# Polysketch attention and a four-expert mix: the first chunk of 128 columns multiplied plainly, and a reordered beginning

**Chip, cores, metric.** One core of a Trainium2 chip. Times are microseconds (us) of device time for one execution. A time quoted for a kernel is the median of its runs. All runs count as fast ones unless a run is called slow. In the lines of the profile PE is TensorE, PEld its loading of weights, DVE VectorE, ACT ScalarE and POOL GpSimd.

## The reference

```python
q, k, v: (4, 4, 1088, 32)      # batch, heads, sequence, head dim
S1, S2:  (8, 32)
domain_probs: (4352, 4);  w1: (4, 128, 1024);  w2: (4, 1024, 128)

phi(x) = outer(S1 x, S2 x)                    # 64 features of each row
kv, z  = phi(k)^T v, sum of phi(k)            # one set for each head
x      = (phi(q) kv) / (phi(q) z + 1e-6)      # heads side by side: (4352, 128)
p      = domain_probs / (domain_probs.sum(-1) + 1e-9)
out    = sum over e of p[:, e] * (relu(x @ w1[e]) @ w2[e])
```

## The kernel before

The 4352 columns of x (transposed: xT is 128 x 4352) are made in units of attention work and used in chunks of expert work. A chunk has 16 steps: 4 experts, each in 4 steps of 256 hidden rows. The engines work as follows.

- **TensorE** multiplies by w1, then two steps later by w2. It also does the attention's projections.
- **ScalarE** does the ReLU from PSUM to SBUF.
- **VectorE** does the subtractions that the second multiplication needs, and all the small steps of the attention.
- **GpSimd** makes the weight sums w2s and gathers the results.

```python
UNITS  = [[256, 416, 416]] + [[384, 352, 352]] * 3         # attention, by batch
CHUNKS = [256, 416, 416] + [512] * 5 + [320, 256, P]       # expert work
ps_h: 3 PSUM buffers "h";  ps_o: "o0", "o1";  ps_f: one "f";  ps_n: "den", "num"
```

All chunks but the last use a scheme of seven half-width products in place of eight. That costs three subtractions a step on VectorE, and four weight sums for each expert on GpSimd:

```python
# first(i): one step of expert e
for j in range(2):
    both(hp, w1[e, ...], xT[chunk])                        # TensorE
    nc.scalar.activation(hd[...], hp, Relu)                # ScalarE
    rectify_and_subtract(...)                              # VectorE: one for j = 0, two for j = 1
    work()
# second(i): seven products of w2 blocks or w2s with the parts of hd
# the last chunk, plain(m): only a transposing Relu, and eight records of 128 columns
```

The next units' attention is a generator of small "pieces". `work()` puts them between the expert steps, at a rate that has each chunk's columns ready in time. The pieces of the queries, in their order:

```python
# queries(b, c, n): transpose of q ... projection into the PSUM buffer "f"
qf = shuffle(f); qf = f + qf                               # VectorE
qb = shuffle(qf)
for x in range(2):
    qa = shuffle(qf)
    for p in range(2):
        qp[p] = qa * qb                                    # VectorE, two SBUF inputs
# attend: den, num on TensorE; transpose, add, reciprocal, transpose, product on VectorE
```

At the beginning, the sketch words S1 and S2 (64-bit numbers) are taken apart on VectorE (19 small operations) and spread by ScalarE and VectorE to `sk` (for keys) and by GpSimd to `sr` (for queries). The keys are transposed, projected and summed, and the first unit's 256 columns pass the attention. Only then can the first expert matmul start.

## Time and profile before

| | before |
|---|---|
| time, median of 3 | 500.53 us (500.36 to 500.74) |
| profiled span | 498.2 us |
| TensorE busy | 98% |
| first key projection / first expert matmul | 6.43 / 16.96 us |

The page, the windows up to 94.72 and the opening are in the prediction below. What belongs to them here are the later windows of the kernel before (from:to, length; then busy time and count of TensorE, weight loads, VectorE, ScalarE, GpSimd; granted clock, DMA share, GB/s):

```profile
140.42:197.61 57.19, 57.19 (x511) 42.40 (x509) 39.07 (x81) 28.30 (x54) 23.25 (x23) 1.00 0.18 52
197.61:478.82 281.21, 281.21 (x2325) 211.84 (x2323) 182.59 (x422) 148.41 (x293) 139.21 (x141) 1.00 0.08 22
```

and its timeline in chunk 1 (start, length, engine, line, operation, out<-in, count; in brackets how long the engine was idle before it and what ended that):

```profile
71.57 0.37 ACT L347 COPY fs<-f 128x256 f32<-128x256 f32 x1 [0.41 <-PE f L177]
72.00 0.45 PE L177 MATMUL f<-sk,kT 128*64 128x64 f32 x8 [0.47 <-ACT fs L347]
```

Busy times of TensorE hide small holes, because the ends of matmuls are modelled. Each stage is set against a price: every matmul record of n columns counted at n x 0.4167 + 1.2 ns (the prediction derives it). A stage's length less its price is its **holes**. They are good to about 0.1 us, because a record that starts at the very cut between two chunks can be counted on either side.

### The profile page before, as it was taken

Reading aid. Unit: us, or ns where it says so; the run is one execution under the profiler, and the core shown is the slowest. Engines: PE = TensorE matmul, PEld = TensorE weight load, DVE = VectorE, ACT = ScalarE, POOL = GpSimd, SP = SyncE. Lnnn points to the kernel's source line nnn. Section 1 sums busy time; section 2 is a strip of 40 time slices with the busy share of each in tenths; the row PEclk is TensorE's granted clock in tenths of the full one; section 3 lists DMA queues with packets and bytes.
Section 4 is the critical chain, followed back from the end, with each engine's and each line's share of the span. In section 5 each row is a group of like instructions: output and inputs, shape, how many; then the busy total and the mean of one; then the engine's idle time right before and its main releaser. Section 6 shows DMA issues by size and latency. Waiting matters only on the chain.

```text
span 498.2 us, 11354 instructions
## 1 busy us (share of the span) xinstructions
PE 489.8 (98%) x4530; PEld 369.4 (74%) x4530; DVE 333.6 (67%) x802; ACT 252.6 (51%) x519; POOL 239.3 (48%) x288
## 2 busy tenths in 40 slices
PE   8799999999999999999999999999999999999997
PEld 5577667777777777777777777777777777788996
DVE  6687868678766685857657646558656557665643
ACT  3255445555554454544545455445455445566662
POOL 6576316444544253444555244344555355665570
PEclk9999999999999999999999999999999999999999
DMA  8950123011002230021002100021001100110000
GB/s 256 348 130 1 59 65 94 1 53 51 2 1 84 63 91 1 2 86 21 1 1 82 27 1 1 2 84 22 2 0 54 22 1 0 45 22 1 16 2 19
DMA packets 29957, 22.65 MB, mean 45 GB/s; under 512 B 20432, under 2 KB 26960, under 8 KB 29520
## 3 DMA queue, kind: packets, MB, share of 16 engines
q1 hardware_dynamic: 28608, 20.98, 14.6%
q10 hardware_dynamic: 1296, 0.94, 0.7%
q8 instruction: 36, 0.59, 0.5%
q14 instruction: 17, 0.14, 0.1%
HBM read 19.61 MB, written 2.31 MB: 44 GB/s over the span
## 4 chain that ended last, share of the span: by engine, by line
PE 97%; DVE 1%; ACT 0%; issue 0%; DVEq 0%
PE h L177 48%; PE o L177 40%; PE f L177 5%; PE den L177 2%; PE num L177 2%; PE h L167 1%; DVE hid L589 1%; DVE qp L416 0%; ACT hid L615 0%; DVE kvz L379 0%; DVE dT L438 0%; DVE rb L446 0%; DVE xT L450 0%; DVE rc L441 0%; ACT fs L347 0%
## 5 line engine op out<-in xcount | busy, mean ns | idle before, releaser
L589 DVE SCALAR_TENSOR_TENSOR hid<-h,hid 128x256 f32<-128x256 f32 (+6 forms) x480 | 214.6, 448 | 144.6 <-ACT hid L615 134.4
L177 PE MATMUL h<-xT,w_sb 128*64 128x512 f32 (+4 forms) x1408 | 299.2, 496 | 2.7 <-DVE xT L450 1.8
L615 ACT ACTIVATE hid<-h 128x512 f32<-128x512 f32 (+3 forms) x320 | 167.2, 523 | 211.7 <-PE h L177 166.9
L177 PE MATMUL o<-hid,w2s 128*64 128x256 f32 (+3 forms) x1280 | 232.0, 342 | 0.0
L177 PE MATMUL o<-hid,w_sb 128*64 128x256 f32 (+3 forms) x960 | 193.2, 342 | 0.0
L177 PEld LDWEIGHTS h<-xT,w_sb 128*64 128x64 f32 x1408 | 148.9, 137 | 53.8 <-issue 3.5
L177 PEld LDWEIGHTS o<-hid,w2s 128*64 128x64 f32 x1280 | 143.8, 137 | 29.7
L731 POOL TENSOR_TENSOR ev<-yz,sh 64x256 f32<-64x256 f32 (+3 forms) x80 | 51.7, 646 | 164.5 <-ACT sh L734 161.5
L177 PEld LDWEIGHTS o<-hid,w_sb 128*64 128x64 f32 x960 | 110.6, 137 | 23.0 <-issue 3.3
L719 POOL TENSOR_TENSOR yz<-ev 128x512 f32<-128x512 f32 (+3 forms) x40 | 44.3, 1108 | 67.0 <-ACT ev L722 66.8
L731 POOL TENSOR_TENSOR ct<-ev 128x512 f32<-128x512 f32 (+3 forms) x40 | 44.1, 1102 | 3.1
L731 POOL TENSOR_TENSOR ct<-ct,gate 128x512 f32<-128x512 f32 (+3 forms) x30 | 33.6, 1119 | 2.3
L731 POOL TENSOR_TENSOR total<-total,ct 128x512 f32<-128x512 f32 (+3 forms) x30 | 33.2, 1108 | 2.4
L416 DVE TENSOR_TENSOR qp<-qa,qb 64x352 f32<-64x352 f32 (+2 forms) x44 | 28.8, 655 | 1.0
L721 ACT COPY ev<-o 128x512 f32<-128x512 f32 (+3 forms) x40 | 20.4, 511 | 9.1 <-PE o L177 8.4
L722 ACT COPY ev<-o 128x512 f32<-128x512 f32 (+3 forms) x40 | 20.5, 512 | 2.4
L358 DVE TENSOR_TENSOR kp<-fs 128x256 f32<-128x256 f32 (+1 forms) x24 | 16.6, 699 | 0.0
L734 ACT COPY sh<-yz 64x256 f32<-64x256 f32 (+3 forms) x40 | 14.6, 366 | 1.5 <-POOL yz L719 0.5
L735 ACT COPY sh<-yz 64x256 f32<-64x256 f32 (+3 forms) x40 | 14.6, 366 | 1.0
L475 DVE STREAM_SHUFFLE qa<-qf 128x352 f32<-128x352 f32 (+2 forms) x22 | 12.6, 573 | 0.0
L177 PEld LDWEIGHTS f<-vx,kp 128*64 128x64 f32 x288 | 11.7, 137 | 1.2
L177 PE MATMUL den<-qp,kvz 128*64 128x352 f32 (+3 forms) x48 | 11.4, 470 | 0.6 <-DVE kvz L379 0.6
(106 smaller groups left out, 238.8 us busy)
## 6 DMA issues: line engine op xcount, KB each, us to landing
w_sb<-in_moe_w_dram SPq DMA_DIRECT2D x8, 512.0 KB, 6.4
gate<-gates SPq DMA_DIRECT2D x3, 1024.0 KB, 4.7
kn<-in_k_dram SPq DMA_DIRECT2D x4, 544.0 KB, 3.9
qn<-in_q_dram SPq DMA_DIRECT2D x4, 544.0 KB, 3.8
vn<-in_v_dram SPq DMA_DIRECT2D x14, 128.0 KB, 4.8
gate<-gates SPq DMA_DIRECT2D x2, 832.0 KB
gate<-gates SPq DMA_DIRECT2D x1, 896.0 KB
out_dram<-ob SPq DMA_DIRECT2D x13, 64.0 KB, 2.0
```

The lines of the kernel that those rows point to most:

```text
L177: nc.tensor.matmul(out(s), weights(s), moving(s), **flags)
L358: eng.tensor_tensor(out=_ap(kps[b], 0, P, 256 * t0 + P * p + 64 * x, [[256, n], [32, 2], [R, 4], [1, R]]), in0=in0, in1=_ap(fss[b], 0, P, ...
L416: nc.vector.tensor_tensor(out=qp[p][64 * x : 64 * x + 64, 0:n], in0=qa[64 * p : 64 * p + 64, 0:n], in1=qb[64 * p : 64 * p + 64, 0:n], op=A ...
L475: nc.vector.stream_shuffle(in_=qf[:, 0:n], out=qa[:, 0:n], mask=mask_a[x])
L589: nc.vector.scalar_tensor_tensor(out=out, in0=src, scalar=0.0, in1=in1, op0=ALU.max, op1=ALU.subtract)
L615: nc.scalar.activation(hd[:, n * j : n * j + n], hp[:, 0:n], ACTF.Relu)
L719: add = lambda out, in0, in1, op=ALU.add: nc.gpsimd.tensor_tensor(out=out, in0=in0, in1=in1, op=op)
L721: nc.scalar.copy(_ap(ev, 0, P, 0, [[2 * w, 2], [1, w]]), _ap(a0, 0, P, 0, two))
L722: nc.scalar.copy(_ap(ev, 0, P, w, [[2 * w, 2], [1, w]]), _ap(a1, 0, P, 0, two))
L731: add = lambda out, in0, in1, op=ALU.add: nc.gpsimd.tensor_tensor(out=out, in0=in0, in1=in1, op=op)
L734: nc.scalar.copy(sh[HP:P, 0:w], yz[0:HP, 0, 0:w])
L735: nc.scalar.copy(sh[0:HP, 0:w], yz[HP:P, 1, 0:w])
```

## The change

Its intent is to start the expert work earlier. The first chunk becomes 128 columns in place of 256, multiplied plainly, so it needs neither subtractions on VectorE nor weight sums before it. The beginning is shortened: sketch words handled side by side, only the first 128 columns of q loaded ahead, gates made later, query factors of both pairs of heads computed side by side in one PSUM buffer. The core of the diff:

```diff
-    QW = 416
+    QW = 480
-    UNITS = [[256, 416, 416]] + [[384, 352, 352]] * 3
-    CHUNKS = [256, 416, 416] + [512] * 5 + [320, 256, P]
+    UNITS = [[P, 480, 480]] + [[384, 352, 352]] * 3
+    CHUNKS = [P, 480, 480] + [512] * 5 + [320, 256, P]
     # loads: dp leaves ScalarE's queue and comes later; v's second half is then the next there
-    qn[0] = load_rows(q, 0, "qn")
+    load_rows(q, 0, "qn", slice(0, P))
     vn[0] = load_v(0, (nc.sync, nc.scalar))
+    # dp, ends (gates of the two plain chunks), then
+    load_rows(q, 0, "qn", slice(P, S))
-    for e in range(2):
+    for e in range(E):
         load_w1(e); load_w2(e)
     # sketch words: 32 x 64 words hold the high and low parts side by side, 15 operations for 19
-        copy = nc.vector.tensor_copy if h // 2 else nc.scalar.copy      # sk
+        nc.scalar.copy(...)
     # start(): query factors
-        fq = [psum(ps_n, "num"), psum(ps_n, "den"), psum(ps_o, "o0")]   # 24 records of 256
+        fq = [psum(ps_o, "o0"), psum(ps_o, "o1")]                       # 32 records of 128
-        make_gates() ... store_gates() ... weight_sums(0)               # no longer in start()
     def plain(m):
-        return m == NC - 1
+        return m in (0, NC - 1)
-            if kq % 2:                      # plain step: ReLU by VectorE and ScalarE in turn
+            if m and kq % 2:                # in chunk 0: all by ScalarE
     # the loop over the steps
-    to_sum = chain.from_iterable(weight_sums(e) for e in range(1, E))
-            if m == 0 and kq > 2:
-                for _ in range(2 if kq < 5 else 1):
-                    next(to_sum, None)
+    to_sum = chain.from_iterable(weight_sums(e) for e in range(E))
+            if i:
+                next(to_sum, None)          # one weight sum a step, from step 1 on
+            if i == 2: gate_quotients()
+            elif i == 5: store_gates(); load_gate(1); load_gate(2); load_batch(1)
     # [cut: gate sums, key_divide's order, the end of a plain chunk]
```

## The prediction

> **What bounds the kernel now.** I read the page first (busy shares, then the chain), then the windows of the stages, then the timeline of the first 20 us.
>
> ```profile
> PE 489.8 (98%) x4530; PEld 369.4 (74%) x4530; DVE 333.6 (67%) x802; ACT 252.6 (51%) x519; POOL 239.3 (48%) x288
> PE 97%; DVE 1%; ACT 0%; issue 0%; DVEq 0%
> ```
>
> TensorE is busy throughout and is 97% of the chain. A change can therefore pay in two ways only: fewer matmul columns, or fewer holes in TensorE. The windows (engine busy times, granted clock, DMA share, GB/s) show where holes are:
>
> ```profile
> 13.50:16.96 3.46, 1.08 (x8) 0.49 (x8) 2.43 (x7) 0.00 (x0) 2.41 (x4) 1.00 1.14 346
> 16.96:46.61 29.65, 28.75 (x341) 21.69 (x342) 23.19 (x68) 16.10 (x44) 16.99 (x25) 1.00 0.51 149
> 46.61:94.72 48.11, 47.64 (x511) 33.53 (x509) 34.87 (x81) 24.17 (x53) 18.66 (x23) 1.00 0.19 57
> 94.72:478.82 384.10, 384.10 (x3209) 290.27 (x3207) 257.10 (x590) 200.66 (x396) 184.87 (x187) 1.00 0.10 27
> ```
>
> The cuts are the first expert matmul (16.96) and the first expert matmul of chunks 1, 2 and 10. From 94.72 on there is no hole at all: 384.10 of 384.10. All that can be won lies before 94.72, mostly before 46.61. The timeline of the opening:
>
> ```profile
> 1.25 5.25 PE L167 MATMUL h<-warm 128*128 128x512 bf16 x14 [1.25 <-DVE warm L139]
> 6.43 2.32 PE L177 MATMUL h<-sk,kT 128*64 128x64 f32 x72
> 8.58 1.03 PE L177 MATMUL num<-qT,sr 128*64 128x256 f32 x8
> 9.45 1.03 PE L177 MATMUL den<-qT,sr 128*64 128x256 f32 x8
> 10.31 1.03 PE L177 MATMUL o<-qT,sr 128*64 128x256 f32 x8
> 11.17 2.27 PE L177 MATMUL f<-vx,kp 128*64 128x66 f32 x72
> 13.52 0.49 DVE L379 TENSOR_TENSOR kvz<-f,own 128x128 f32<-128x128 f32 x2 [0.73 <-PE f L177]
> 14.06 0.65 PE L177 MATMUL den<-qp,kvz 128*64 128x256 f32 x4 [0.62 <-DVE kvz L379]
> 14.76 0.45 DVE L438 STREAM_TRANSPOSE dT<-den 128x256 f32<-128x256 f32 x1 [0.76 <-PE den L177]
> 14.92 0.72 POOL L498 TENSOR_TENSOR w2s<-w_sb,w2s 128x256 f32<-128x256 f32 x1
> 15.24 0.42 DVE L441 TENSOR_SCALAR rc<-dT 128x8 f32<-128x8 f32 x1
> 15.94 0.45 DVE L446 STREAM_TRANSPOSE rb<-rc 128x256 f32<-128x256 f32 x1
> 16.48 0.42 DVE L450 TENSOR_TENSOR xT<-num,rb 128x256 f32<-128x256 f32 x1
> 16.96 0.87 PE L177 MATMUL h<-xT,w_sb 128*64 128x256 f32 x6 [1.82 <-DVE xT L450]
> ```
>
> TensorE runs without a break from the warm-up to 13.4, so that part is bound by its own columns, not by the sketch words on VectorE. After that comes a serial chain of small VectorE steps, 13.52 to 16.96.
>
> **A price for a matmul.** In the trace matmuls come in pairs on the two halves of the array, two records of n columns starting 7 ns apart. Start to start of the pairs is 0.2155 us at n = 256, 0.109 at 128, 0.0575 at 64. So a record costs about n x 0.4167 + 1.2 ns. Summed over each chunk this gives 45.68 us for chunk 2 (measured 45.70) and 27.29 for chunk 0 (measured 29.65), so chunk 0 has 2.36 us of holes. Chunk 1 has 0.91.
>
> **What the Trainium skill says.** "TensorE: Matmul & The Clock Gate", section "Wait — 56ns, not 53.3ns?", gives N / 2.4 GHz + about 2.5 ns between warm matmuls; the trace agrees (0.2155 us for a pair of 256). The same page, "What's actually happening", says that the array starts at half clock until it has been busy for some 3.4 us; here the warm-up matmuls go from one every 0.43 us to one every 0.216 us at about 5.5 us. "SBUF — State Buffer", section "SBUF: two separate sides", says that VectorE and GpSimd share a port pair as an exclusive lock, taken by a VectorE operation of two SBUF inputs or in a two-port mode, against a GpSimd one. The trace agrees: the line rc above, 8 columns, took 0.42 us and ended 0.03 us after the GpSimd w2s that began at 14.92; rc takes 0.16 elsewhere. It happens to the query products too:
>
> ```profile
> 28.16 0.57 DVE L416 TENSOR_TENSOR qp<-qa,qb 64x416 f32<-64x416 f32 x1
> 29.42 1.04 DVE L416 TENSOR_TENSOR qp<-qa,qb 64x416 f32<-64x416 f32 x1
> 29.28 0.72 POOL L498 TENSOR_TENSOR w2s<-w_sb 128x256 f32<-128x256 f32 x1
> 34.87 0.65 PE L177 MATMUL h<-xT,w_sb 128*64 128x256 f32 x4 [0.42 <-DVE hid L589]
> ```
>
> Two such collisions (at 29.4 and 33.6) delay the ReLU-subtract behind them and make holes of 0.31 and 0.73 us in TensorE: 1.04 of chunk 0's 2.36. Another 0.77 lies at 18.4 to 20.0, where the first steps wait for rectified data.
>
> **The change, part by part.**
>
> *1. Before the expert work, to the start of the chain.* Joining the sketch words turns 19 VectorE operations into 15, but dependent ones follow each other at 0.14 to 0.2 us instead of 0.09, so s_T comes at about 4.6 for 4.79. All eight sk copies are now on ScalarE: 4 heads x 0.32, ready at about 6.0 for 5.52. VectorE is free for kT earlier, but k landed at 5.16 only, so kT's first part is there at 5.9 to 6.1 for 6.20. The 14 warm-up matmuls stay and hold TensorE until 6.43. So nothing is won here: start 6.43.
>
> *2. TensorE 6.43 to 13.4.* Key projections: 2.15, unchanged. Query factors: 24 records of 256 (2.59) become 32 of 128 (16 pairs x 0.109 = 1.745): -0.84. Key sums: 2.07, unchanged. End of the sums 12.6 for 13.44. This needs the inputs in time. sr on GpSimd: 4 copies of 64 elements (0.23 + 0.057 between them) and 8 of 128 (estimate from 0.203 at 32 and 0.229 at 64: 0.28 + 0.057) = 3.85, from 4.7 to about 8.5; needed at 8.58 and 9.0. The gate sums no longer lie between them. The values: with only 128 columns of q ahead of them (64 KB for 544) v lands some 1.4 us sooner than 9.37, so the first value copy, now ahead of the second fs, does not hold ScalarE at 8.0. The last key product ends at 10.5 and is needed at 11.8.
>
> *3. The chain.* kvz: denominators need only the first of the two now, 0.30 for 0.54. den: two pairs of 128, 0.48 for 0.70. dT at 128 columns: slope between 256 (0.45) and 352 (0.54) is 0.94 ns a column, so 0.33 for 0.45; rb the same; xT 0.31 for 0.43. rc may collide with GpSimd again (0.16 to 0.42). In all 12.66 -> 13.0 -> 13.48 -> 13.84 -> 14.1 -> 14.5 -> 14.9 -> first expert matmul at 15.2. That is 1.76 earlier.
>
> *4. Columns after it.* The second multiplication of 128 columns costs 8 records of 128 a step for 7: 16 steps x 128 x 0.4167 ns = +0.85. Of the attention, 128 columns move behind the first expert matmul: 4 records (+0.21) and 8 records (+0.43) of 128. 96 records fewer: -0.11. Together +1.38.
>
> *5. Holes in chunk 0.* The subtractions go, so VectorE makes no hole there. Each step is 0.87 of TensorE. ScalarE does one transposing ReLU of 128x256, 0.645 in the last chunk of the kernel before: it keeps up. But the next 480 columns must pass VectorE in 16 short steps (15.5 us, not 29.65). Their numerator matmuls come after 11 first and 8 second halves and the projection: 15.2 + 19 x 0.436 + 0.81 = about 24.3. VectorE: transposes from 15.3, gate quotients 1.2, shuffle from 17.65, add, two shuffles (0.65 to 0.69 each) to 20.3, gate transpose and first expert sum to 21.0, four products of 0.65 and a shuffle of 0.69 to about 24.3. No slack, and meanwhile GpSimd runs 16 weight sums of 0.73 back to back: each product may wait up to one of them. I take 0.35 for each of four: 1.4 us of hole, for 2.36 now. Change -0.96. Then xT of the 480 columns is there about 3 us before chunk 1 needs it.
>
> Chunk 1 on: same columns, nothing of note. The gates' later making is hidden: they are first read when chunk 1's sums are gathered, and the last chunk's quotients are off the path.
>
> Sum: -1.76 + 1.38 - 0.96 = -1.34. 500.53 - 1.34 = **499.2 us**.
>
> **The rivals.**
>
> *The numerator wait takes the place of the holes.* If each product waits for a whole weight sum (4 x 0.7 = 2.8) and GpSimd is always first, chunk 0 has 3 us of hole: 500.8. For it: the 1.04 and 0.92 us products; GpSimd was less busy then (16.99 of 29.65). Against: at 28.16 the product won and w2s waited.
>
> *No wait there.* If VectorE gets ahead, chunk 0 has some 0.2: 497.9.
>
> *The opening does not get shorter.* If sr, v or the first w1 (now queued behind the rest of q and the gates, estimate 11.8) come late, TensorE idles before 13, and +1.38 is left: 499.5 to 501.3. For it: sr has 0.1 us to spare by my count. Against: w1 has 3 us.
>
> *The warm-up was not the bound.* If it had been the words, 0.2 more would be won; the unbroken matmuls at 6.43 speak against it.
>
> **Range and chances.** The terms I am least sure of are the chain (0.5) and the hole of chunk 0 (1.3). 8 in 10: 497.4 to 501.0. A gain or loss of 2% would be 10 us, more than all holes before 94.72; 1% each for these.
>
> **What would show it.** Right: the key projections start at 6.4 again; key sums end near 12.6; first expert matmul near 15.2; chunk 1's first near 32; from there on the timeline is the old one, shifted. Step 5 shows as a gap of TensorE before the denominators of the second unit, released by qp, with products well over 0.65 beside w2s. Wrong: a gap before the query factors (sr late), a first fs or vx copy held by v's DMA, expert matmuls released by a weight load, or holes within chunks 1 and 2 that were not there before.

## The result, and the profile after

| | median | runs | ratio to before | span of the trace |
|---|---|---|---|---|
| before | 500.54 us | 6 (499.58 to 501.46) | | 498.2 |
| after | 501.36 us | 6 (500.25 to 502.54) | 1.0019 [0.9999, 1.0038] | 499.2 |

Ratios, here and below, are the mean time of one kernel's fast runs over that of the other's of the same rounds, so not quite the ratio of the medians. The bracket is a 95% interval. The time is within 2%, as was foretold with 0.98, but no gain is seen where 1.34 us was foretold, and 501.36 lies outside the range.

The page of the changed kernel: engines' busy time, and the chain that ended last by engine.

```profile
PE 490.8 (98%) x4442; PEld 367.8 (74%) x4442; DVE 326.5 (65%) x749; ACT 250.7 (50%) x491; POOL 229.8 (46%) x264
...
PE 96%; DVE 3%; issue 0%; ACT 0%; DVEq 0%; ACTq 0%
```

VectorE has 7 us less to do, yet its share of the chain went from 1% to 3%: so VectorE now ends more of TensorE's waits. Where, the windows of the changed kernel show, cut at the first expert matmul of chunks 0, 1, 2, 3 and 4:

```profile
13.47:15.49 2.02, 0.66 (x8) 0.42 (x8) 1.47 (x7) 0.00 (x0) 0.00 (x0) 1.00 1.08 360
15.49:33.24 17.75, 17.23 (x254) 14.56 (x255) 13.96 (x29) 10.09 (x16) 13.34 (x17) 1.00 0.91 296
33.24:88.02 54.78, 53.91 (x503) 40.18 (x501) 36.65 (x80) 25.35 (x51) 12.70 (x12) 1.00 0.18 49
88.02:140.11 52.09, 52.09 (x378) 38.53 (x376) 38.60 (x89) 26.27 (x49) 24.64 (x24) 1.00 0.09 26
140.11:198.49 58.38, 57.92 (x510) 38.68 (x508) 39.41 (x81) 28.40 (x54) 24.55 (x23) 1.00 0.19 52
198.49:479.71 281.22, 281.22 (x2326) 211.85 (x2323) 182.39 (x420) 148.39 (x293) 138.61 (x138) 1.00 0.09 22
```

From chunk 4 on nothing changed: 281.22 for 281.21. With the price taken off each length:

| stage | before: length = price + holes | after: length = price + holes |
|---|---|---|
| to the first expert matmul | 16.96 | 15.49 |
| chunk 0 | 29.65 = 27.29 + 2.36 | 17.75 = 16.14 + 1.60 |
| chunk 1 | 48.11 = 47.21 + 0.91 | 54.78 = 52.86 + 1.92 |
| chunk 2 | 45.70 = 45.68 + 0.02 | 52.10 = 52.08 + 0.01 |
| chunk 3 | 57.19 = 56.86 + 0.33 | 58.38 = 57.33 + 1.05 |

So the start gained 1.47, the price went up by 1.38 (177.04 to 178.41, before rounding), chunk 0's holes shrank by 0.76, chunk 1's grew by 1.01 and chunk 3's by 0.72. The sum is +0.9, which is the difference of the two spans.

**The opening.** The changed kernel's timeline:

```profile
1.25 5.63 PE L176 MATMUL h<-warm 128*128 128x512 bf16 x14 [1.25 <-DVE warm L135]
5.25 1.30 DVE L318 STREAM_TRANSPOSE kT<-kn 128x512 f32<-128x512 f32 x2 [0.52 <-DMA kn<-in_k_dram]
6.81 2.32 PE L186 MATMUL h<-sk,kT 128*64 128x64 f32 x72
8.96 1.92 PE L186 MATMUL o<-qT,sr 128*64 128x128 f32 x32
10.71 2.27 PE L186 MATMUL f<-vx,kp 128*64 128x66 f32 x72
13.12 0.49 DVE L382 TENSOR_TENSOR kvz<-f,own 128x128 f32<-128x128 f32 x2 [1.64 <-PE f L186]
13.47 0.44 PE L186 MATMUL den<-qp,kvz 128*64 128x128 f32 x4 [0.49 <-DVE kvz L382]
...
15.49 1.53 PE L186 MATMUL h<-xT,w_sb 128*64 128x128 f32 x24 [1.36 <-DVE xT L454]
```

Read it against the opening of before: the query factors take 1.75 from their start to the next group's (8.96 to 10.71) where three groups took 2.59, and no input is late. From the first key projection to the first expert matmul it is now 8.68, for 10.53. But the first key projection itself starts at 6.81, not 6.43.

**Chunk 0.** VectorE's products for unit 1 beside GpSimd's weight sums, and the denominators that wait for them:

```profile
21.20 2.07 DVE L420 TENSOR_TENSOR qp<-qa,qb 64x480 f32<-64x480 f32 x2
...
21.61 1.15 POOL L502 TENSOR_TENSOR w2s<-w_sb,w2s 128x256 f32<-128x256 f32 x1
...
24.08 2.22 DVE L420 TENSOR_TENSOR qp<-qa,qb 64x480 f32<-64x480 f32 x2
...
24.64 1.14 POOL L502 TENSOR_TENSOR w2s<-w_sb 128x256 f32<-128x256 f32 x1
...
25.24 1.72 PE L186 MATMUL den<-qp,kvz 128*64 128x480 f32 x3 [0.43 <-DVE qp L420]
```

The four products took 0.96, 1.10, 1.11 and 1.08 us; one alone takes 0.65. The weight sums beside them took 1.15 and 1.14 instead of 0.73. Each engine waits for the other in turn: the first product ends at 22.16, a weight sum at 22.75, the second product at 23.27, the next sum at 23.87. TensorE has holes of 0.60 and 0.70 us ahead of the two halves of the denominators, which wait for these products.

**Chunk 1.** VectorE, then TensorE, in the first steps of chunk 1:

```profile
35.29 0.41 DVE L592 SCALAR_TENSOR_TENSOR hid<-h,hid 128x240 f32<-128x240 f32 x1 [3.67 <-ACT hid L618]
35.62 0.70 DVE L469 STREAM_SHUFFLE qf<-f 128x480 f32<-128x480 f32 x1
36.35 0.66 DVE L471 TENSOR_TENSOR qf<-f,qf 128x480 f32<-128x480 f32 x1
36.93 1.09 DVE L592 SCALAR_TENSOR_TENSOR hid<-h,hid 128x480 f32<-128x480 f32 x2
...
40.43 0.64 DVE L420 TENSOR_TENSOR qp<-qa,qb 64x480 f32<-64x480 f32 x1
40.99 0.34 DVE L657 SCALAR_TENSOR_TENSOR end<-o,ends,end 128x128 f32<-128x128 f32 x1
...
38.16 1.83 PE L186 MATMUL h<-xT,w_sb 128*64 128x480 f32 x8 [0.29 <-ACT hid L618]
41.38 0.63 PE L186 MATMUL o<-hid,w_sb 128*64 128x240 f32 x4 [0.58 <-DVE end L657]
```

Two holes begin here. Ahead of 38.16 (0.56 us by the price) the next h needs one of three PSUM buffers. By the program, that buffer is free when VectorE has done the two subtractions of 36.93 to 38.02, whose ReLU was ready at 36.00. They stood behind a shuffle and an add of unit 2's query. The bracket names a ReLU of ScalarE, because that one ended 0.03 us later. Ahead of 41.38 (0.75) the second multiplication of chunk 1 needs the accumulator "o1", which chunk 0's last expert still holds. VectorE reads it out at 40.99, behind a product. Note the 3.67 in the first line: VectorE had been idle since 31.62, while the work that crowds chunk 1 was not handed to it yet.

**Chunk 3.** A hole of 0.69 in the changed kernel is the wait that the kernel before showed in chunk 1 at 72.00:

```profile
170.94 0.37 ACT L348 COPY fs<-f 128x256 f32<-128x256 f32 x1 [0.33 <-PE f L186]
171.36 0.45 PE L186 MATMUL f<-sk,kT 128*64 128x64 f32 x8 [0.46 <-ACT fs L348]
```

### The profile page after: what moved, and what is told of

It is laid out like the page before. It is cut to its first block, busy times and chain, and to the rows that moved or that the text cites. A ratio compares the mean times of both kernels' runs of the same rounds, so it can differ in the third digit from the quotient of the medians.

```text
span 499.2 us, 11045 instructions
## 1 busy us (share of the span) xinstructions
PE 490.8 (98%) x4442; PEld 367.8 (74%) x4442; DVE 326.5 (65%) x749; ACT 250.7 (50%) x491; POOL 229.8 (46%) x264
## 4 chain that ended last, share of the span: by engine, by line
PE 96%; DVE 3%; issue 0%; ACT 0%; DVEq 0%; ACTq 0%
PE h L186 48%; PE o L186 39%; PE f L186 5%; PE den L186 2%; PE num L186 1%; PE h L176 1%; DVE qp L420 1%; DVE hid L592 1%; DVE qa L479 0%; DVE qf L469 0%; DVE qb L474 0%; DVE qf L471 0%; DVE end L657 0%; ACT hid L618 0%; ACT fs L348 0%
## 5 line engine op out<-in xcount | busy, mean ns | idle before, releaser
L592 DVE SCALAR_TENSOR_TENSOR hid<-h,hid 128x256 f32<-128x256 f32 (+6 forms) x432 | 203.7, 472 | 149.0 <-ACT hid L618 140.7
L618 ACT ACTIVATE hid<-h 128x512 f32<-128x512 f32 (+3 forms) x288 | 158.3, 550 | 202.4 <-PE h L186 169.9
L186 PE MATMUL o<-hid,w2s 128*64 128x256 f32 (+3 forms) x1152 | 220.9, 355 | 0.0
L186 PE MATMUL o<-hid,w_sb 128*64 128x256 f32 (+3 forms) x864 | 185.0, 356 | 0.6 <-DVE end L657 0.6
L186 PEld LDWEIGHTS o<-hid,w2s 128*64 128x64 f32 x1152 | 131.5, 137 | 31.7 <-issue 0.6
L733 POOL TENSOR_TENSOR ev<-yz,sh 64x256 f32<-64x256 f32 (+3 forms) x72 | 48.6, 675 | 159.0 <-ACT sh L736 156.3
L186 PEld LDWEIGHTS o<-hid,w_sb 128*64 128x64 f32 x864 | 101.4, 137 | 21.1 <-issue 1.6
L610 ACT ACTIVATE hid<-h 128x256 f32<-128x256 f32 x24 | 15.3, 655 | 18.7 <-PE h L186 18.2
L186 PE MATMUL o<-w_sb,hid 128*64 128x128 f32 x256 | 24.0, 273 | 0.0
L186 PEld LDWEIGHTS o<-w_sb,hid 128*64 128x64 f32 x256 | 19.9, 137 | 1.7 <-issue 1.5
```

What stands on the lines that cost most here:

```text
L186: nc.tensor.matmul(out(s), weights(s), moving(s), **flags)
L592: nc.vector.scalar_tensor_tensor(out=out, in0=src, scalar=0.0, in1=in1, op0=ALU.max, op1=ALU.subtract)
L610: nc.scalar.activation(turned, src, ACTF.Relu)
L618: nc.scalar.activation(hd[:, n * j : n * j + n], hp[:, 0:n], ACTF.Relu)
L733: add = lambda out, in0, in1, op=ALU.add: nc.gpsimd.tensor_tensor(out=out, in0=in0, in1=in1, op=op)
```

## The experiments

The theory after the result has four parts: (a) chunk 0's holes are the port that VectorE and GpSimd share; (b) chunk 1's holes come from the order in which VectorE gets the pieces and the subtractions; (c) chunk 3's hole is the one buffer "f", met by a new interleaving; (d) the first key projection is held by the warm-up matmuls or by k. The main rival to (a) to (c): any wait that is taken away only moves to the next one. In the expectations the runs have names: e3_key_psum is run 3, c1_three run 7, c2_three_early run 8 and c4_warm12 run 10. "Excess" is what is called holes here.

### 1. The weight sums of experts 1 to 3 later

```diff
-            if i:
+            if 0 < i < 5:
                 next(to_sum, None)
+            elif i == 16:      # a tiny copy that needs chunk 1's first columns, then all the rest
+                nc.gpsimd.tensor_copy(late[:, :], xT[:, START[1] : START[1] + 1])
+                for _ in to_sum: pass
```

> The changed kernel, with the weight sums of experts 1 to 3 (12 GpSimd operations) held back until the attention of the first 480 columns is written; everything else unchanged. In the changed kernel the four query products of that unit took 0.96, 1.10, 1.11 and 1.08 us beside these sums, and TensorE stood 0.60 and 0.70 us before the two halves of the denominator matmuls. Theory (port lock): the products fall to 0.65 us each, the two gaps (1.30) shrink to under 0.3, chunk 0 lasts 16.5 us for 17.75, the span falls by 1.0 to 1.3 us. Rival (VectorE is simply behind, whatever GpSimd does): products stay near 1 us or the gap stays above 0.9, span unchanged. Second rival: the sums now collide with chunk 1's query work and the gain is given back there, span within 0.3 us of the changed kernel's 499.2.

Measured: 499.63 us (498.63 to 500.63), ratio 0.9984 [0.9963, 1.0005], span 497.8. The products and the denominators in its timeline:

```profile
21.43 1.31 DVE L420 TENSOR_TENSOR qp<-qa,qb 64x480 f32<-64x480 f32 x2
23.54 1.34 DVE L420 TENSOR_TENSOR qp<-qa,qb 64x480 f32<-64x480 f32 x2
24.88 1.08 PE L186 MATMUL den<-qp,kvz 128*64 128x480 f32 x4
```

Four products of 0.64 to 0.65 us, no bracket before the denominators, and holes of 0.06 in chunk 0 for 1.60. That is far outside the scatter: in the traces of runs 2, 3 and 5, which leave chunk 0's sums and products as they are, chunk 0 has holes of 1.42 to 1.87. So it is shown that the weight sums cause chunk 0's holes; that they do it through a shared port is the reason that fits these durations, but no run isolates the port. The gain was not given back: chunk 1 has 1.82 of holes for 1.92, chunk 3 the same 1.05. In the times, 499.63 against 501.36, the intervals of the two ratios overlap.

### 2. No attention pieces in chunk 1's first three steps

```diff
             def work():
+                if m == 1 and kq < 3:
+                    return
```

> The changed kernel, with no query pieces interleaved in the first three steps of chunk 1. In the changed kernel chunk 1 has gaps of 0.56 us (before the third expert matmul group of 480) and 0.75 us (an accumulation that waits for chunk 0's last gated sum on VectorE, which stood behind a query product). Theory (VectorE's order): both vanish, the excess of chunk 1 over the column price falls from 1.92 to about 0.7, span falls by about 1.2 us. Rival: the gaps come from ScalarE's ReLU and the PSUM buffers and stay, or they come back when the pieces are crowded later in the chunk; span unchanged within 0.3.

Measured: 502.66 (501.84 to 503.36), ratio 1.0044 [1.0025, 1.0063], span 500.5. Chunk 1's holes fell to 0.53, but chunk 2's rose from 0.01 to 2.00 and chunk 3's to 1.22. Chunk 0 had 1.87, which is scatter, since the edit does not touch it. The timeline of chunk 2 in this kernel:

```profile
103.80 1.59 DVE L420 TENSOR_TENSOR qp<-qa,qb 64x384 f32<-64x384 f32 x1
...
105.45 0.87 PE L186 MATMUL den<-qp,kvz 128*64 128x384 f32 x4 [1.10 <-DVE qp L420]
```

The holes of chunk 1 go when the pieces do, as (b) says, but holding the pieces back moves them: what follows comes later, and a product of 1.59 us, beside a GpSimd operation, now makes the denominators wait. The rival is right for this remedy.

### 3. Another PSUM buffer for the second key projection

```diff
-            key_project(b, gi, psum(ps_f, "f"))
+            key_project(b, gi, psum(ps_n, "den") if gi == 1 else psum(ps_f, "f"))
```

> The changed kernel, with the second of the three key projections of each later batch put into the PSUM tile of the denominators instead of the one tile that all three share. In the changed kernel TensorE stood 0.69 us at 171.4 before a key projection that waited for ScalarE to empty that tile (the kernel before had a gap of 0.64 at 72.0 in the same place of its first later batch). Theory (single buffer, hit by chance of the interleaving): the gaps before key projections go, 0.7 to 1.0 us less in all, chunk 3's excess 1.05 falls to about 0.35. Rival (ScalarE is late with the whole group): the gap moves to the next user of the tile, span unchanged.

Measured: 500.82 (499.63 to 501.46), ratio 1.0012 [0.9992, 1.0033], span 497.8. The copy that TensorE had waited for, now in the other buffer:

```profile
169.17 1.10 PE L186 MATMUL den<-sk,kT 128*64 128x64 f32 x29
...
170.47 0.37 ACT L348 COPY fs<-den 128x256 f32<-128x256 f32 x1 [0.33 <-PE den L186]
```

Nothing waits for it any more. Chunk 3's holes went from 1.05 to 0.20; chunk 1's are 1.87, as good as unchanged. Part (c) is shown for the trace. In the median time it is 0.5 us, with overlapping intervals.

### 4. The kernel before with the new sizes alone

```diff
-    QW = 416
-    UNITS = [[256, 416, 416]] + ...
-    CHUNKS = [256, 416, 416] + ...
+    QW = 480
+    UNITS = [[128, 480, 480]] + ...
+    CHUNKS = [128, 480, 480] + ...
```

> The kernel before with only its sizes changed: units and chunks of 128, 480, 480, first chunk still by the seven-product scheme, old opening and gates. If the shorter opening of the change comes mainly from the 128 columns, the first expert matmul comes at about 15.5 us here too (15.49 in the changed kernel, 16.96 before). If it comes from the reordering, it stays above 16. For chunk 0 I expect VectorE to be the bound (three subtractions of a step plus the query steps, about 1.2 us for 0.82 of TensorE): holes of 4 to 6 us there, total 501.5 to 504.

Measured: 509.71 (fast runs 509.58 to 509.77; the profiled run was a slow one, 583.72 at a clock of 0.849), ratio 1.0185 [1.0167, 1.0203]. So only its times count, and not the lengths in its trace. Its fast runs all had a clock of 0.997; against runs of the kernel before at that clock (500.94 in the same rounds) the sizes cost about 9 us when chunk 0 still needs its subtractions and weight sums. This was well above what was expected. Against runs of the complete change at 0.996 and 0.997 (502.43 and 502.54), the plain multiplication and the new beginning together are worth about 7 us at these sizes. How that splits between the two is not settled by this run. Nor is what was asked of it, whether the shorter opening comes from the sizes or from the reordering: in the slow trace the first expert matmul comes at 16.45, but TensorE's clock had fallen to 0.85 by then.

### 5. Another accumulator for chunk 0's last expert

```diff
-                acc[m] = psum(ps_o, f"o{e % 2}")
+                acc[m] = psum(ps_n, "num") if (m, e) == (0, 3) else psum(ps_o, f"o{e % 2}")
```

> The changed kernel, with one edit: chunk 0's last expert accumulates in the PSUM tile of the numerators, which is idle then, not in the tile that chunk 1's first expert needs next. Theory: the gap of 0.75 us at 41.4 in the changed kernel is chunk 1's accumulation waiting for VectorE to read chunk 0's last sum, which stands behind a query product; it goes, the gap of 0.56 at 38.2 stays, chunk 1's excess 1.92 falls to about 1.2, the span by 0.7. Rival: the gap is set by the ReLU-subtract data, and another wait ends at the same time; excess unchanged within 0.2.

Measured: 501.33 (500.67 to 502.31), ratio 1.0019 [1.0002, 1.0035], span 499.3. The hole ahead of 41.4 is gone, and chunk 1's holes are 1.91 for 1.92: one of 0.63 now lies ahead of unit 2's denominators at 47.03, behind these:

```profile
46.00 1.65 PE L186 MATMUL den<-qp,kvz 128*64 128x480 f32 x3
...
46.32 0.65 DVE L420 TENSOR_TENSOR qp<-qa,qb 64x480 f32<-64x480 f32 x1
```

The accumulator was only where the lateness of VectorE came to light. By itself another accumulator is worth nothing.

### 6. The edit of 3 in the kernel before

> The kernel before with the same edit as e3_key_psum (second key projection of a later batch in another PSUM tile). Theory: the wait for the shared tile is not the change's own, it hits whichever batch the interleaving places badly: here the gap of 0.64 at 72.0 goes and chunk 1's excess 0.91 falls to about 0.3, the span to about 497.3 to 497.6 (with the opening as lucky as in the first trace). Rival: the wait belongs to the changed kernel's pacing, and here nothing moves (span 498.2 within 0.3).

Measured: 499.3 (498.91 to 500.79), ratio 0.9982 [0.9965, 1.0], span 497.3. Chunk 1's holes went from 0.91 to 0.22. So the wait for the buffer "f" isn't of the change's making. By the lists of waits of the first 200 us, each kernel meets it once there, at another place (0.5 us both times).

### 7 and 8. Edits 1, 3 and 5 together; then also query pieces in the end of chunk 0

Run 7 is the three edits. Run 8 adds this, which hands unit 2's query pieces to VectorE from chunk 0's end on, when unit 1's 19 pieces are done:

```diff
-                credit[0] = min(credit[0] + rate / 2, 2)
+                more = 1 if m == 0 and done[0] >= 19 else rate / 2
+                credit[0] = min(credit[0] + more, 2)
```

> The changed kernel with three edits together: weight sums of experts 1 to 3 later, second key projection in another PSUM tile, chunk 0's last expert in the numerator tile. If the three causes are separate, their gains add: excess of chunk 0 about 0.1 (was 1.60), chunk 1 about 1.0 (1.92), chunk 3 about 0.2 (1.05), span 499.2 - 1.5 - 0.9 - 0.8 = 496.0 with the opening of the first trace, up to 0.4 more if the array's clock rises late; time about 0.9925 to 0.995 of the kernel before. Rival: the faster stage only makes the next one wait, and the sum is under half of that.

> As c1_three, with query pieces of the second unit of 480 taken as soon as the first is done, in the last steps of chunk 0, where VectorE idles (30.8 to 35.3 in the changed kernel) rather than in the first steps of chunk 1. Theory: the gap of 0.56 at 38.2 came from a shuffle and an addition ahead of chunk 1's subtracts; it goes, 0.5 us less than c1_three. Rival: the pieces stay ahead of or beside the subtracts anyway, or the projection of the unit now makes TensorE wait in chunk 0; no gain or a loss of 0.5.

Measured: run 7 498.39 (498.11 to 500.0), ratio 0.9964 [0.9948, 0.998], holes 0.06, 1.78 and 0.20 in chunks 0, 1 and 3. The gains of chunks 0 and 3 add; chunk 1 misses its forecast of 1.0, as run 5 had already done. Run 8 496.83 (496.2 to 498.37), ratio 0.9933 [0.9916, 0.9949], holes 0.12, 0.14 and 0.25. The windows of run 8, for chunks 0, 1 and 3:

```profile
15.17:31.54 16.37, 16.37 (x255) 14.93 (x257) 12.53 (x32) 9.52 (x16) 6.59 (x11) 1.00 0.92 291
31.54:84.53 52.99, 52.99 (x502) 40.02 (x500) 35.26 (x80) 26.39 (x51) 18.28 (x20) 1.00 0.23 64
...
136.62:194.11 57.49, 57.49 (x511) 42.74 (x509) 39.26 (x81) 28.38 (x54) 24.43 (x23) 1.00 0.19 53
```

and what TensorE still waits for in the first 200 us (engine, line, releaser: total, times, longest), first of the changed kernel, then of run 8:

```profile
...
PE o L186 <- DVE end L657: 0.6, 1, 0.6
...
PE f L186 <- ACT fs L348: 0.5, 1, 0.5
PE den L186 <- DVE qp L420: 0.4, 1, 0.4
PE h L186 <- ACT hid L618: 0.3, 1, 0.3
```

```profile
PE h L186 <- DVE xT L454: 1.4, 1, 1.4
...
PE h L186 <- DVE kT L318: 0.7, 1, 0.7
PE den L186 <- DVE kvz L382: 0.5, 1, 0.5
```

Only waits of the opening are left. From run 7 to run 8 one edit takes chunk 1's holes from 1.78 to 0.14. So part (b) is shown, by using VectorE's idle stretch at the end of chunk 0 instead of postponing.

### 9. The early pieces alone

> The changed kernel with only the edit that takes the second unit's query pieces in the last steps of chunk 0 (where VectorE idles from 30.8 to 35.3). Theory: chunk 1's holes have one cause, VectorE being behind when the chunk begins, so this edit alone takes its excess from 1.92 to under 0.5, with chunk 0's 1.60 and chunk 3's 1.05 as they were; span about 497.7 for 499.2. Rival: the accumulator that waits for chunk 0's last sum (0.75) is a cause of its own, and excess stays at 0.9 or above.

Measured: 499.85 (499.7 to 500.97), ratio 0.9995 [0.9973, 1.0016], span 498.1. Chunk 1's holes are 1.32: the hole ahead of 38.2 is gone, but about 0.9 is left where the accumulator waits:

```profile
40.39 0.63 PE L186 MATMUL o<-hid,w_sb 128*64 128x240 f32 x4 [0.60 <-DVE end L657]
```

So the accumulator is a cause of its own. Alone the two edits take away 0.01 (run 5) and 0.60 (here); when the early pieces join the accumulator, from run 7 to run 8, 1.64 goes. Runs 7 and 8 also have the edits of runs 1 and 3, and the two edits of chunk 1 without these were not run: that the two suffice is likely, not shown.

### 10 to 12. What holds the first key projection

Run 10 is run 8 with 12 warm-up matmuls in place of 14, run 11 with 10. Run 12 is run 10 with the second half of v issued behind k on the same queue:

```diff
-    vn[0] = load_v(0, (nc.sync, nc.scalar))
+    vn[0] = load_v(0, (nc.sync, nc.sync))
```

> c2_three_early with 12 warm-up matmuls for 14. The traces so far have the clock rising anywhere between the seventh and the fourteenth of them. Prediction's theory (the warm-up holds the first key projection): it comes 0.2 to 0.4 us sooner where the clock rises late, time 0.2 to 0.4 lower than c2_three_early. Rival (in the changed opening the sketch copies, all on ScalarE, or k's landing hold it at 6.5 at the earliest): nothing won where the clock rises early, first projection not before 6.5.

> c2_three_early with 10 warm-up matmuls. They end at 5.6 at the latest, so the warm-up can't hold the first key projection in any phase of the clock: its start then shows what else does. Warm-up theory: 6.1 to 6.2. Rival (ScalarE's eight sketch copies and k): 6.5 to 6.9 as in the traces where the clock rose early. If the array falls back or stays at half clock, the key projections take up to 2 us longer, and the time is higher than c2_three_early's by up to 2.

> c4_warm12 with all of v's first rows issued from the sync queue, behind k and the first 128 columns of q; in the change half of them go out from ScalarE's queue at 1.65 us, at the same time as k. In five of the traces with the changed opening k landed at 5.65 to 5.97 and the first key projection came 0.88 us after it; with the old opening k landed at 5.03 and 5.16. Theory (v beside k delays k): k lands at 5.2 or sooner, the first key projection at 6.0 to 6.1 (6.4 if the clock rises late), the first expert matmul near 14.9, time 0.2 to 0.5 lower than c4_warm12. Rival (k's landing only scatters): k lands within 5.2 to 6.0 as before, nothing won. Second rival: v now comes late for its copies (wanted at 8.3) and TensorE waits for the key sums.

| run | k landed | last warm-up started | key projection | expert matmul | time | ratio to before |
|---|---|---|---|---|---|---|
| before | 5.16 | 6.12 | 6.43 | 16.96 | 500.54 | |
| after | 5.23 | 6.51 | 6.81 | 15.49 | 501.36 | 1.0019 |
| run 1 | 5.37 | 6.74 | 7.05 | 15.72 | 499.63 | 0.9984 |
| run 5 | 5.97 | 5.48 | 6.86 | 15.50 | 501.33 | 1.0019 |
| run 6 | 5.03 | 5.65 | 6.14 | 16.74 | 499.3 | 0.9982 |
| run 8 | 5.65 | 5.47 | 6.53 | 15.17 | 496.83 | 0.9933 |
| run 10 | 5.70 | 5.92 | 6.58 | 15.26 | 496.57 | 0.9922 [0.9908, 0.9936] |
| run 11 | 5.43 | 5.06 | 6.31 | 15.29 | 497.53 | 0.9949 [0.9918, 0.9979] |
| run 12 | 5.14 | 5.77 | 6.16 | 14.80 | 496.52 | 0.9921 [0.9908, 0.9935] |

In the changed opening the key projection starts either 0.31 after the last warm-up matmul has started (after, run 1) or 0.88 to 0.89 after k has landed (runs 5, 8, 10, 11). Which of the two it is depends on when the clock rises and on when k lands. Runs 3, 7 and 9 wait for k too, by the same 0.88 to 0.89; run 2 starts 0.39 after its last, slow warm-up. Run 12 fits neither: it starts 0.39 after the last warm-up, which was a fast one, and 1.02 after k; there the last sketch copy on ScalarE ends at 6.06, 0.10 before it, but what held it is not shown. The interval of the warm-up matmuls falls from 0.43 to 0.216 us anywhere between about 4.2 us (runs 5 and 8) and after the last one (run 2, where all 14 ran slowly, the last from 6.77; and run 11, where all 10 did and the first key projections too: they took about 0.3 longer). In two openings VectorE's transpose waits for k; in run 8 TensorE waits for that transpose, in run 12 it does not. First run 8, then run 12:

```profile
5.67 1.30 DVE L318 STREAM_TRANSPOSE kT<-kn 128x512 f32<-128x512 f32 x2 [0.97 <-DMA kn<-in_k_dram]
6.53 0.59 PE L186 MATMUL h<-sk,kT 128*64 128x64 f32 x13 [0.68 <-DVE kT L318]
```

```profile
5.16 1.30 DVE L318 STREAM_TRANSPOSE kT<-kn 128x512 f32<-128x512 f32 x2 [0.47 <-DMA kn<-in_k_dram]
6.16 0.94 PE L186 MATMUL h<-sk,kT 128*64 128x64 f32 x25
```

In the kernel before, v's second half was issued behind dp, from 2.04 us. In the changed one it goes out from 1.65, beside k. There k landed at 5.23 to 5.97 (ten traces), in the two fast traces of the old opening at 5.16 and 5.03, and in run 12, with v behind k, at 5.14. The Trainium skill, "DMA: Bandwidth & Descriptors", section "Issuing engines are not separate DMA queues", says that transfers issued by different engines run on the same 16 DMA engines and interleave; these times agree. But run 12 is one trace: its expert work starts 0.46 us before run 10's, its span is 494.4 for 494.9, and its time is equal (496.52 and 496.57). v did not come late for its copies: from the key projection to the expert matmul run 12 takes 8.64, as run 8 does. That v's order shortens the time is not shown.

Run 11's first key projection came at 6.31, between its two forecasts. Its median is above run 10's because three of its runs had a clock of 0.997 (498.3 to 500.5). At 1.0 it had 496.48 to 496.71. So the number of warm-ups, between 14 and 10, is not shown to matter either. Runs 10 and 12 are the fastest of all: 496.5 us, some 4 us below the kernel before and 5 below the changed one.

## Why the prediction was wrong

Step by step, with what the runs showed in its place:

- **"So nothing is won here: start 6.43"** (step 1): failed by 0.38 us. The step counted on the warm-up to hold TensorE to 6.43, as in one trace. In the runs the warm-up's end moves with the rise of the clock (its last matmul starts between 5.47 and 6.77 in runs with 14 of them). Where it ends early, k is the bound, which landed up to 0.8 later in the changed opening than in the trace of before. The 6.43 itself came from one trace with a late warm-up. In run 6, with the same old opening, the warm-up ended earlier, and the first key projection came at 6.14, 0.86 after its transpose, which stood directly behind VectorE's last sketch copy (5.09 to 5.25; k had landed at 5.03). So in the old opening the rival "the warm-up was not the bound" holds in run 6; in the changed opening the transpose waited for k in every trace, and shorter work on the words won nothing.
- **Steps 2 and 3, columns and chain**: right. From the first key projection to the first expert matmul 8.77 was foretold (6.43 to 15.2), and 8.68 measured. No input came late.
- **Step 4, price**: right, +1.38 both ways.
- **Step 5, chunk 0**: right in the mechanism, and run 1 shows it. A wait of 0.35 for each of four products was foretold; they waited 0.41 on average (1.06 less 0.65). The holes were 1.60 for 1.4; with 1.42 to 1.87 in other traces of the same chunk 0, so close a hit is partly luck.
- **"Chunk 1 on: same columns, nothing of note"**: this is the step that failed. Holes grew by 1.01 in chunk 1 and 0.72 in chunk 3. It counted TensorE's columns and left out who feeds it. In the kernel before, chunk 0 was 29.65 us long, and unit 2's pieces spread from there on. In the changed one chunk 0 lasts 17.75, and its end leaves VectorE idle for 3.67 us. Then chunk 1's subtractions of 480 columns, unit 2's pieces and the read-out of chunk 0's last sum come at once. Runs 7 to 9 show it: with another accumulator in place, pieces moved into the idle stretch take 1.64 of chunk 1's holes away. In chunk 3 it is a wait on a single PSUM buffer that both kernels have (runs 3 and 6), met at a new place by the moved interleaving: the kernel before had it in chunk 1, the changed one has it in chunk 3. With this wait taken out of both kernels, chunk 1 has 1.87 for 0.22 and chunk 3 0.20 for 0.2 to 0.3. So what the change itself added after chunk 0 is all in chunk 1, about 1.65 us of waits on VectorE. The reading "no hole at all" after 94.72, from modelled busy times, had also hidden that chunk 3 had 0.33 of holes before.

The miss in the trace is 2.21 us: start 0.29, chunk 0 0.20, chunk 1 1.01, chunk 3 0.72, less 0.01 of price. The prediction's last part named "holes within chunks 1 and 2 that were not there before" as what would show it wrong; they came in chunks 1 and 3.

The first rival, the numerator wait in chunk 0, gave a time near the measured one (500.8) for a wrong reason: its holes of 3 us were 1.60. Had only the total been looked at, it would have seemed right.

The gain that the change was made for is there in part: the start is 1.47 earlier, chunk 0's own holes are smaller, and 1.38 of price is paid back for it by design. The rest was lost in new waits on VectorE and on PSUM buffers. Without these waits the kernel is 0.7 to 0.8% faster than the kernel before (runs 8, 10 and 12). Part of that is not the change's: the other buffer for key projections helps the kernel before too (run 6). Against run 6, in the same rounds, run 8 is 0.5% faster (496.83 for 499.3).

Open: how much of the first key projection's delay is v's early issue and how much is chance; how experiment 4's 9 us divide; and whether the chunk 3 wait could be avoided by interleaving alone.

## What to carry to other kernels

When a chunk at the front of a pipelined kernel is made shorter, work out again when each helper engine gets its work, not only what the main engine has to do: the same pieces in less time are a burst, and an idle stretch just ahead of the burst is where they belong. Undo waits in combination, since a buffer freed alone can show nothing while the engine that held it is still late (run 5). And where two events race in an opening, look at several traces before naming the bound.

## What the Trainium skill lacked or had wrong

- "SBUF — State Buffer", section "SBUF: two separate sides", has the exclusive lock right (four products 0.96 to 1.11 us beside weight sums, 0.64 to 0.65 without: run 1). It lacks what two queues of such operations do to each other: they take turns, and both lose, a product 0.41 us on average and a weight sum 0.42 (1.15 for 0.73). So a product grew by less than a whole weight sum each time.
- "TensorE: Matmul & The Clock Gate", section "What's actually happening", says that the point of the rise varies by ±500 ns with the phase of a window of 3.4 us, and elsewhere in the section that the number of slow matmuls differs from run to run. Here the same first matmul at 1.25 us was followed by the rise at about 4.2 us in runs 5 and 8 and after 6.77 in run 2, all with 14 warm-ups: over 2.5 us apart. The second statement fits, the first is too narrow.
- No page read says what goes with a mean granted clock just below 1: runs at 0.995 to 0.997 took 0.7 to 1.9 us of 500 more (one 3.8), before and after the change, and that is as much as most of the effects here.
- "DMA: Bandwidth & Descriptors", section "Issuing engines are not separate DMA queues", gives the rule but no size: with two issues of 128 KB of v on another queue, the first 0.24 us behind 544 KB of k (1.65 and 1.41 us), k landed at 5.23 to 5.97 us; with these issued later, at 5.03 to 5.16.
